# Retention plus two MoE layers on one core: one chunk's state products in a row, and the query decay multiplied into the output

## The chip, the cores and the metric

The kernel runs on one core of one Trainium2 chip. The metric is the device time of one execution in microseconds (us), the median of the runs shown. The engines are named as in the profile: PE is TensorE, PEld its weight loads, DVE is VectorE, ACT is ScalarE, POOL is GpSimd, SP is the engine that issues most loads.

## The reference, cut to what matters

Three layers follow each other: decayed attention ("retention") without softmax, an MoE-like layer with a rational activation, and a gated layer with RMS normalisation. The change lies in the first.

```python
batch, n_heads, seq, head_dim = (4, 8, 576, 64)
scores = scale * np.matmul(q, k.transpose(0, 1, 3, 2))
gamma = 1.0 - 2.0 ** (-5.0 - np.arange(H, dtype=np.float32))
Dmat = np.where(rel >= 0, gamma[:, None, None] ** rel[None, :, :], 0.0)   # rel = pos[:, None] - pos[None, :]
ret = scores * Dmat[None, :, :, :]
return np.matmul(ret, v)
```

The result, as 2304 tokens of 512 values, goes through `_moe_ref` (512 to 2048 to 512) and `_moe2_ref` (512 to 1536 to 512).

## The kernel before

The attention is cut into 20 steps: 4 batches (`b`) of 5 chunks (`c`), chunks 0 to 3 of 128 positions and chunk 4 of 64. Eight heads are held as four pairs (`p`), the two heads of a pair (`e`) on the two halves of the 128 partitions. The decay gamma^(i-j) is split in two powers. `prep_q` multiplies q in place by gamma^i (the table `gq`, with the scale in it), and `dmk` holds the mask times gamma^-j. A running state `SS` of each head carries all earlier chunks.

One step `i` of `att_jobs` issues:

- `att_add` (DVE, L280 or L278): adds the last chunk's state product out of PSUM to the state; `att_decay` (ACT, L227) makes the decayed copy for the chunk after.
- `att_scores` for step i+1, once for each `e` (PE, L202, four products): scores into a PSUM bank; DVE multiplies them by `dmk` into `ret` (L207).
- `att_out` (PE): for each pair a state product with 128 weight columns (L238, if c > 0) and then the two value products, with 64 weight columns each, into the two halves of the bank (L243). The first three chunks (the tokens of the first tile of the next layer) are split into two fp32r parts by ACT (L217) and DVE (L218); the other 17 are copied out of PSUM by ACT (L251) into `xe` and stored to DRAM by a DMA from ACT's queue (L252).
- `att_state` (PE, L264): the chunk's state product.
- `prep_q(i + 2)` on POOL (L188), and `prep_k(i + 1)` on POOL (L193), which multiplies k by its decay. `prep_q` of steps 0 and 1 is done by DVE at the start.

Every attention matmul is fp32, and the profile shows each as two instructions. Steps 0 to 2 run alone at the start (`att_jobs("h", 0, P0)`). The other 17 are spread over the first token tile of the second layer (`hook(j)`), between its own matmuls: `m1_up` (L312 to L314) and `m1_down` (L321, L322, L325), with their elementwise work on DVE, ACT and POOL (L331 to L369). In the same stretch the weights of that layer are unpacked from 64-bit floats (`Weights.step`): ACT L141 and L142, DVE L143, L144 and L148, POOL L151, ACT L157, and DVE or POOL L158; the result `w` is what `m1_up` and `m1_down` load. A scheduler that estimates times orders the instructions of each engine, so an edit in one place moves instructions in others. During the spread steps scores, output and state products take turns in two PSUM banks (`bank("a")`).

From 265 us on no attention work is left: the rest of the second layer and the third layer run.

## Time and profile before

| what | us |
|---|---|
| median of the runs | 1054.47 (1054.26 to 1058.04) |
| the profiled execution, its own time | 1060.39 |
| its span, first to last instruction | 1058.5 |
| PE busy / DVE busy / ACT busy / POOL busy, whole span | 1015.0 / 620.5 / 555.8 / 449.1 |
| granted TensorE clock, mean of the span | 0.954 |

How to read it: the shares of the whole span say little, since the attention lies in the first quarter only. There DVE is nearly as busy as PE, and the granted clock is well under 1. A PE that is "busy" at a granted clock of 0.5 (1.2 GHz) does half of what it does at 1.0 (2.4 GHz). A matmul's duration is a pipeline's latency: what a group of matmuls costs is read from the start of its first to the start of what comes after.

### The profile page before, as it was taken

The numbers are of one execution on the slowest core, as the hardware profiler recorded it, in microseconds if no ns is written. First come the engines' busy times: TensorE is split into PE (matmuls) and PEld (weight loads), VectorE is DVE, ScalarE is ACT, GpSimd is POOL, SyncE is SP. The second block draws the span as 40 slices with busy tenths as digits, with TensorE's granted clock in tenths as the row PEclk, the third lists the DMA queues.
The fourth block names the chain that finished last, engine by engine and source line by source line (L and its number), as shares of the span: only waits on it lengthen the run. The fifth ranks groups of instructions, "written<-read, shape, count | busy, mean of one in ns | idle before, by whom it ended". The sixth has DMA issues, their size and how long they took to land. (4 is left out here: it accounts for less than half of the span.)

```text
span 1058.5 us, 14977 instructions
## 1 busy us (share of the span) xinstructions
PE 1015.0 (96%) x5726; PEld 934.6 (88%) x5726; DVE 620.5 (59%) x1022; ACT 555.8 (53%) x1091; POOL 449.1 (42%) x397
## 2 busy tenths in 40 slices
PE   8988999989999999999999989898999999999998
PEld 6776877779999999999999889888999999999997
DVE  5598889896767768677688885765311211211211
ACT  2474566569778787787877665454311211211111
POOL 4474867577456474564755745554300100100000
PEclk7687889799999999999999999999999999999999
DMA  6554656431010010100102343332300100100000
GB/s 252 181 172 144 228 149 225 147 114 60 30 31 2 30 31 31 30 2 31 31 21 70 110 135 118 116 114 86 120 1 1 60 1 1 46 1 1 31 1 30
DMA packets 37592, 78.91 MB, mean 75 GB/s; under 512 B 5904, under 2 KB 21392, under 8 KB 37520
## 3 DMA queue, kind: packets, MB, share of 16 engines
q1 hardware_dynamic: 16416, 47.72, 13.5%
q10 hardware_dynamic: 21104, 30.23, 9.1%
q8 instruction: 45, 0.74, 0.3%
q14 instruction: 27, 0.22, 0.1%
HBM read 64.57 MB, written 13.37 MB: 74 GB/s over the span
## 5 line engine op out<-in xcount | busy, mean ns | idle before, releaser
L440 PE MATMUL bank<-x,w 128*128 128x384 f32 x528 | 178.4, 338 | 12.8 <-DVE sg L446 11.2
L442 PE MATMUL bank<-x,w 128*128 128x384 f32 x528 | 178.4, 338 | 0.0
L441 PE MATMUL bank<-x,w 128*128 128x384 f32 x528 | 178.2, 337 | 0.0
L446 DVE TENSOR_TENSOR sg<-sg,bank 128x384 f32<-128x384 f32 x72 | 39.8, 552 | 221.8 <-PE bank L442 221.6
L312 PE MATMUL bank<-x,w 128*128 128x384 f32 x384 | 134.3, 350 | 4.0 <-DVE u L350 4.0
L151 POOL TENSOR_TENSOR ft<-ft,raw 128x512 int32<-128x512 int32 x68 | 97.3, 1430 | 94.9 <-DVE ft L148 56.5
L348 POOL TENSOR_TENSOR q<-q,ah 128x384 f32<-128x384 f32 x96 | 101.9, 1062 | 81.8 <-ACT q L344 75.1
L322 PE MATMUL bank<-g,w 128*128 128x384 f32 x384 | 125.5, 347 | 7.9 <-DVE w L158 7.9
L314 PE MATMUL bank<-x,w 128*128 128x384 f32 x384 | 131.8, 343 | 0.6 <-DVE w L158 0.6
L313 PE MATMUL bank<-x,w 128*128 128x384 f32 x384 | 130.6, 340 | 0.0
L321 PE MATMUL bank<-g,w 128*128 128x384 f32 x384 | 125.1, 345 | 2.2 <-ACT g L368 1.1
L369 POOL TENSOR_TENSOR g<-u,g 128x384 fp32r<-128x384 f32 x96 | 101.3, 1056 | 60.1 <-ACT g L368 32.2
L218 POOL TENSOR_TENSOR x<-xr,x 128x384 fp32r<-128x384 f32 x44 | 47.8, 1096 | 162.9 <-ACT x L217 162.9
L440 PEld LDWEIGHTS bank<-x,w 128*128 128x128 f32 x528 | 99.9, 189 | 17.6 <-DVE sg L446 12.5
L445 ACT ACTIVATE sg<-bank 128x384 f32<-128x384 f32 x72 | 35.1, 488 | 143.8 <-PE bank L442 142.2
L441 PEld LDWEIGHTS bank<-x,w 128*128 128x128 f32 x528 | 99.9, 189 | 2.7
L442 PEld LDWEIGHTS bank<-x,w 128*128 128x128 f32 x528 | 100.0, 189 | 0.3
L448 ACT ACTIVATE y<-sg 128x384 fp32r<-128x384 f32 x72 | 37.6, 523 | 107.6 <-DVE sg L446 103.9
L325 PE MATMUL bank<-g,w 128*128 128x384 f32 x384 | 86.2, 341 | 0.0
L349 DVE TENSOR_TENSOR u<-u,bank 128x384 f32<-128x384 f32 x96 | 52.9, 551 | 52.4 <-ACT u L345 51.6
L322 PEld LDWEIGHTS bank<-g,w 128*128 128x128 f32 x384 | 73.8, 195 | 9.8 <-DVE w L158 9.5
L312 PEld LDWEIGHTS bank<-x,w 128*128 128x128 f32 x384 | 73.7, 192 | 8.4 <-DVE u L350 5.8
(101 smaller groups left out, 2210.8 us busy)
## 6 DMA issues: line engine op xcount, KB each, us to landing
raw<-in_w_out_dram SPq DMA_DIRECT2D x28, 512.0 KB, 3.5
xb<-in_qkT_dram ACTq DMA_DIRECT2D x17, 512.0 KB, 4.0
raw<-in_w_in_dram SPq DMA_DIRECT2D x16, 512.0 KB, 4.5
kv<-in_kv_dram ACTq DMA_DIRECT2D x14, 512.0 KB, 4.5
raw<-in_w_gate_dram SPq DMA_DIRECT2D x12, 512.0 KB, 3.5
raw<-in_w_val_dram SPq DMA_DIRECT2D x12, 512.0 KB, 3.5
xn_d<-x SPq DMA_DIRECT2D x6, 768.0 KB, 3.8
xr<-xn_d ACTq DMA_DIRECT2D x24, 192.0 KB, 2.4
```

The lines of the kernel that those rows point to most:

```text
L151: pool.tensor_tensor(out=ft, in0=ft, in1=lo, op=ALU.add)
L312: pe.matmul(out=h, lhsT=w[:, 0, ks], rhs=x[:, 0, k], start=(k == 0), stop=False)
L313: pe.matmul(out=h, lhsT=w[:, 0, ks], rhs=x[:, 1, k], start=False, stop=False)
L314: pe.matmul(out=h, lhsT=w[:, 1, ks], rhs=x[:, 0, k], start=False, stop=(k == KD - 1))
L321: pe.matmul(out=acc[m], lhsT=w[:, 0, ms], rhs=g[:, 0], start=(j == 0), stop=False)
L322: pe.matmul(out=acc[m], lhsT=w[:, 1, ms], rhs=g[:, 0], start=False, stop=False)
L325: pe.matmul(out=acc[m], lhsT=w[:, 0, ms], rhs=g[:, 1], start=False, stop=(j == J1 - 1))
L348: pool.tensor_tensor(out=q, in0=q, in1=ah, op=ALU.mult)
L369: pool.tensor_tensor(out=g[:, 1], in0=u, in1=g[:, 0].bitcast(F32), op=ALU.subtract)
L440: pe.matmul(out=t, lhsT=w[:, 0, ks], rhs=x[:, 0, k], start=(k == 0), stop=False)
L441: pe.matmul(out=t, lhsT=w[:, 0, ks], rhs=x[:, 1, k], start=False, stop=False)
L442: pe.matmul(out=t, lhsT=w[:, 1, ks], rhs=x[:, 0, k], start=False, stop=(k == KD - 1))
```

## The change

`prep_q` is gone: q stays as loaded, and so scores and the state product lack the factor gamma^i of their query position. The output lies with its positions along the free dimension as q did, so the factor is multiplied in where the output leaves PSUM: one DVE multiplication by `gq` out of the bank into `xe`. It takes the place of ACT's copy for 17 chunks, and stands ahead of the split for the first three. In `att_out` the four state products come first and then the eight value products. All groups of a chunk lie in one bank, and only the first product clears it.

```diff
-    def prep_q(i, eng):
-        if i < len(steps):
-            q = qk_b[i % 3][:, 0]
-            eng.tensor_tensor(out=q, in0=q, in1=gq, op=ALU.mult)
-
...
-        for p in range(NP):
-            if c > 0:
+        if c > 0:
+            for p in range(NP):
                 pe.matmul(
                     out=o[:, p, 0:n], lhsT=SS[c % 2][:, p].rearrange("p a d -> p (a d)"),
-                    rhs=q[:, p, 0:n], start=True, stop=False,
+                    rhs=q[:, p, 0:n], start=(p == 0), stop=False, skip_group_check=True,
                 )
+        for p in range(NP):
             for e in range(2):
                 pe.matmul(
                     out=o[64 * e:64 * e + 64, p, 0:n], lhsT=v[0:n, 2 * p + e],
-                    rhs=rets[i, e][0:n, p, 0:n], start=(c == 0), stop=True,
+                    rhs=rets[i, e][0:n, p, 0:n], start=(c == 0 and p == 0), stop=(p == NP - 1),
+                    skip_group_check=True,
                 )
         t0 = b * SEQ + c * CH
+        xo = xe[:, :, 0:n]
+        dve.tensor_tensor(out=xo, in0=o[:, :, 0:n], in1=gq[:, :, 0:n], op=ALU.mult)
         if t0 < TA:
-            split_x(0, slice(0, KD), t0, n, o[:, :, 0:n], dve)
+            split_x(0, slice(0, KD), t0, n, xo, dve)
         else:
-            act.activation(out=xe[:, :, 0:n], in_=o[:, :, 0:n], func=ACTF.Copy)
-            act.dma_start(out=x1_d[:, :, t0:t0 + n], in_=xe[:, :, 0:n])
+            act.dma_start(out=x1_d[:, :, t0:t0 + n], in_=xo)
...
-            prep_q(i + 2, pool)
             prep_k(i + 1, pool)
...
-    prep_q(0, dve)
...
-    prep_q(1, dve)
```

PE, step 2 of the start (`S_115` is the state, `ret` the masked scores, the second number a product's output). Before:

```order
L238 MATMUL bank_105<-xb,S_115 128x128
L243 MATMUL bank_105<-ret,kv_112 64x128 x2
L238 MATMUL bank_105<-xb,S_115 128x128
L243 MATMUL bank_105<-ret,kv_112 64x128 x2
L238 MATMUL bank_105<-xb,S_115 128x128
L243 MATMUL bank_105<-ret,kv_112 64x128 x2
L238 MATMUL bank_105<-xb,S_115 128x128
L243 MATMUL bank_105<-ret,kv_112 64x128 x2
```

PE, the same step after the change (L197 is the scores' line there, L262 the state product's, L233 and L239 what L238 and L243 were):

```order
L197 MATMUL bank_102<-xb 128x128 x4
L197 MATMUL bank_103<-xb 128x128 x4
L262 MATMUL bank_104<-kv_112 64x64 x8
L233 MATMUL bank_105<-xb,S_115 128x128 x4
L239 MATMUL bank_105<-ret,kv_112 64x128 x8
```

Seven changes between 128 and 64 weight columns have become one.

POOL at the start, before (L188 is the multiplication of q, L193 that of k, L151 a weight's unpacking):

```order
L188 TENSOR_TENSOR xb<-xb,gx 128x512
L193 TENSOR_TENSOR kv_112<-kv_112,gk 128x512
L151 TENSOR_TENSOR ft<-ft,raw 128x512
L188 TENSOR_TENSOR xb<-xb,gx 128x512
L151 TENSOR_TENSOR ft<-ft,raw 128x512
L193 TENSOR_TENSOR kv_110<-kv_110,gk 128x512
L188 TENSOR_TENSOR xb<-xb,gx 128x512
L151 TENSOR_TENSOR ft<-ft,raw 128x512
L188 TENSOR_TENSOR xb<-xb,gx 128x512
L151 TENSOR_TENSOR ft<-ft,raw 128x512
```

POOL there after the change (L188 is now k's multiplication):

```order
L188 TENSOR_TENSOR kv_111<-kv_111,gk 128x512
L188 TENSOR_TENSOR kv_112<-kv_112,gk 128x512
L151 TENSOR_TENSOR ft<-ft,raw 128x512 x2
L188 TENSOR_TENSOR kv_110<-kv_110,gk 128x512
L151 TENSOR_TENSOR ft<-ft,raw 128x512
L188 TENSOR_TENSOR kv_112<-kv_112,gk 128x512
L151 TENSOR_TENSOR ft<-ft,raw 128x512
```

The unpacking steps no longer stand behind a multiplication that waits for a load of q.

DVE after the change, around the third and fourth output (L246 is the new multiplication, L213 the split, L202 the scores' multiplication):

```order
L158 TENSOR_TENSOR w<-ft,w 128x512
L246 TENSOR_TENSOR gx<-bank_105,gx 128x512
L144 TENSOR_SCALAR ft<-ft 128x512
L202 TENSOR_TENSOR ret<-bank_102,dmk 128x512
L143 TENSOR_SCALAR ft<-ft 128x512
L148 SCALAR_TENSOR_TENSOR ft<-raw,ft 128x512
L202 TENSOR_TENSOR ret<-bank_105,dmk 64x4x64
L213 TENSOR_TENSOR x<-gx,x 128x4x128
L144 TENSOR_SCALAR ft<-ft 128x512
L246 TENSOR_TENSOR gx<-bank_104,gx 128x512
```

The bank now leaves by DVE, in line between a weight's steps and the scores.

## Rows read from the trace of the kernel before

**Rows 1.** Busy time by stretch: PE, PEld, DVE, ACT, POOL, PEclk, DMA share, GB/s.
```profile
0.00:47.00 47.00, 43.47 (x225) 30.49 (x225) 22.03 (x41) 16.87 (x34) 19.43 (x26) 0.64 0.62 217
47.00:240.00 193.00, 175.39 (x1206) 143.51 (x1204) 169.80 (x243) 120.20 (x240) 128.67 (x98) 0.87 0.54 172
...
265.00:558.00 293.00, 289.17 (x1649) 285.27 (x1648) 214.30 (x392) 228.09 (x457) 165.20 (x165) 1.00 0.08 26
```

**Rows 2.** Waits of PE, 47 to 265 us: total us, times, longest.
```profile
PE bank L322 <- DVE w L158: 7.9, 5, 3.3
PE bank L238 <- DVE S L280: 4.9, 3, 2.7
```

**Rows 3.** Waits of DVE, 47 to 240 us.
```profile
DVE ret L207 <- PE bank L202: 12.1, 9, 3.3
DVE S L280 <- PE bank L264: 4.3, 4, 1.4
```

**Rows 4.** Timeline of PE, step 2: start us, us; first rows of steps 2 and 3.
```profile
32.96 0.79 PE L238 MATMUL bank<-xb,S 128*128 128x128 f32 x2
...
38.37 0.80 PE L238 MATMUL bank<-xb,S 128*128 128x128 f32 x2
```

**Rows 5.** Timeline of PE, value products and scores each in a row.
```profile
14.51 1.97 PE L243 MATMUL bank<-ret,kv 128*64 128x128 f32 x16
16.41 2.07 PE L202 MATMUL bank<-xb 64*128 64x128 f32 x8
18.42 0.91 PE L264 MATMUL bank<-kv 128*64 128x64 f32 x12
```

**Rows 6.** Timeline of PE, a chunk at full clock and what follows it.
```profile
104.65 0.38 PE L238 MATMUL bank<-xb,S 128*128 128x128 f32 x2
...
107.69 0.67 PE L202 MATMUL bank<-xb 64*64 64x64 f32 x8
```

**Rows 7.** Groups by line and form, 0 to 420 us: count, busy us, mean ns, idle before.
```profile
L188 POOL TENSOR_TENSOR xb<-xb,gx 128x512 f32<-128x512 f32 x18 | 25.3, 1403 | 25.5 <-DMA xb<-in_qkT_dram 23.6 <-PE bank L202 1.3 <-DVE w L158 0.6
...
L207 DVE TENSOR_TENSOR ret<-bank,dmk 128x512 f32<-128x512 f32 x32 | 21.9, 686 | 23.7 <-PE bank L202 12.4 <-PE bank L243 8.2 <-POOL dmk L532 3.1
...
L251 ACT ACTIVATE gx<-bank 128x512 f32<-128x512 f32 x13 | 7.7, 590 | 11.5 <-PE bank L243 11.5
...
L207 DVE TENSOR_TENSOR ret<-bank,dmk 64x256 f32<-64x256 f32 x8 | 3.3, 414 | 2.4 <-PE bank L202 2.3
...
L218 DVE TENSOR_TENSOR x<-bank,x 128x512 fp32r<-128x512 f32 x3 | 2.1, 684 | 0.0
```

**Rows 8.** The same view: DVE operations with and without a PSUM operand.
```profile
L148 DVE SCALAR_TENSOR_TENSOR ft<-raw,ft 128x512 int32<-128x512 int32 x32 | 30.4, 950 | 0.6
...
L144 DVE TENSOR_SCALAR ft<-ft 128x512 int32<-128x512 int32 x32 | 25.9, 808 | 0.5
...
L158 DVE TENSOR_TENSOR w<-ft,w 128x512 fp32r<-128x512 f32 x24 | 25.4, 1060 | 1.8 <-ACT w L157 1.8
...
L332 DVE SCALAR_TENSOR_TENSOR bank<-q,bank 128x384 f32<-128x384 f32 x42 | 23.5, 559 | 0.7
...
L332 DVE SCALAR_TENSOR_TENSOR q<-q,ah 128x384 f32<-128x384 f32 x16 | 16.1, 1007 | 0.1
```

**Rows 9.** Line L144 alone, 0 to 265 us: duration ns, shortest, median, longest.
```profile
L144 DVE TENSOR_SCALAR ft<-ft x32: 410/724/1498, 15.7 to 231.5; 128x512 int32<-128x512 int32 x32
```

**Rows 10.** Timeline of POOL: a multiplication of q that waits, and what follows.
```profile
43.27 1.27 POOL L188 TENSOR_TENSOR xb<-xb,gx 128x512 f32<-128x512 f32 x1 [6.53 <-DMA xb<-in_qkT_dram]
44.50 1.30 POOL L151 TENSOR_TENSOR ft<-ft,raw 128x512 int32<-128x512 int32 x1
```

**Rows 11.** Two stretches at half clock, columns as in rows 1.
```profile
17.00:27.00 10.00, 10.00 (x53) 7.86 (x52) 6.12 (x10) 2.12 (x5) 5.12 (x4) 0.50 0.41 118
187.00:200.00 13.00, 12.49 (x48) 10.05 (x49) 9.58 (x14) 7.24 (x15) 7.48 (x6) 0.50 0.44 160
```

**Rows 12.** Stores from L252: us from issue to landing.
```profile
DMA to landing us min/median/max: 2.2/3.7/6.3
```

**Rows 13.** Timeline of PE: first matmul of the second layer.
```profile
42.99 0.67 PE L312 MATMUL bank<-x,w 128*128 128x384 f32 x1
```

## Prediction

> **What bounds the kernel now.** I first cut the span by stage with the busy times by stretch [rows 1], since the change touches only the attention, which ends before 265 us. From 265 to 558 us PE is busy 289.17 of 293.00 us at a granted clock of 1.00: that stretch is PE's own and the change leaves its work alone. Of the two stretches with attention, the first (0 to 47 us) is PE's too: PE is busy 43.47 us while DVE is busy 22.03 and ACT 16.87, at a clock of 0.64. The second (47 to 240 us) belongs to nobody alone: PE is busy 175.39 of 193.00 us, so idle 17.6, and DVE 169.80, so idle 23.2. The waits say the same from both sides: PE waits for unpacked weights (7.9 us) and for the state's addition (4.9 us) [rows 2], and DVE waits for scores (12.1 us) and state products (4.3 us) [rows 3]. In such a stretch a saving on one engine reaches the end only in part, and work added to DVE costs in part.
>
> **PE: the products in a row.** In step 2, at half clock, the state products start at 32.96 and those of step 3 at 38.37, so a chunk of four state and eight value products takes 5.41 us [rows 4]. Without state products between them the eight value products take 16.41 - 14.51 = 1.90 us, and four score products, which also load 128 weight columns, 18.42 - 16.41 = 2.01 us [rows 5]. Four state products in a row are not in the trace. The score products are the nearest row, so a chunk would take 2.01 + 1.90 = 3.91 us, which is 1.50 less. As a bound from the other side, if alternating cost nothing the saving would be zero, but then rows 4 and 5 could not differ by 1.50, so I leave a loss out. At full clock a chunk takes 107.69 - 104.65 = 3.04 us [rows 6]; the saving lies between half of 1.50 (it scales with the clock) and 1.50, and I take 0.9, near the half, because 3.04 itself is nearer to half of 5.41 than to all of it.
>
> Sixteen of the twenty chunks have state products: twelve of 128 positions and four of 64. Three of the twelve fall in the first stretch, at half clock: 3 x 1.50 = 4.5 us. The other nine lie between 47 and 240 us, where the mean clock is 0.87 [rows 1]; at 1.1 us each that is 9.9 us. For the four short ones no row shows the parts; they get half, 0.6 us each, 2.4 us. So PE loses 4.5 us of work at the start and 12.3 us in the mixed stretch.
>
> **POOL: no multiplication of q.** Eighteen operations of 1403 ns go, 25.3 us [rows 7]. POOL is not the bound (128.67 of 193.00 us), but two things hang on it. First, these operations wait for loads of q, 23.6 us in all [rows 7], and what is queued behind them waits too: at 43.27 us one has waited 6.53 us for its load, and a weight's unpacking step runs only after it, at 44.50 [rows 10]. That step leads to the weights for which PE waits 7.9 us [rows 2]. I give back 3 us of these 7.9; the bounds are 0 and 7.9.
>
> Second, POOL's work lengthens DVE's. L144 takes between 410 and 1498 ns for the same shape [rows 9]. The same L332 takes 559 ns with a PSUM operand and 1007 ns with both in SBUF [rows 8]. Against 410 ns for L144, 559 for L332 and, for the two-operand lines L148 and L158 of 128x512, the 686 ns of L207 [rows 7], the surplus is 32 x 398 + 16 x 448 + 32 x 264 + 24 x 374 ns = 12.7 + 7.2 + 8.4 + 9.0 = 37.3 us. The removed 25.3 us are 17% of POOL's 19.43 + 128.67 us [rows 1]; by that share DVE gets 6.4 us back, some 5.4 of them after 47 us.
>
> The Trainium skill ("SBUF — State Buffer", section "Who interferes with whom") says that VectorE operations with two SBUF inputs, or in a two-port mode, and GpSimd operations that read SBUF lock each other out for a whole instruction. Rows 8 and 9 agree in kind. If every removed operation had blocked DVE for its whole length, 25.3 us instead of 6.4 would come back, and the forecast below would be some 8 us lower.
>
> **DVE: the multiplication out of PSUM.** It has one PSUM and one SBUF operand, as L207 has in the same shape: 686 ns, and 414 ns for the 64-position form [rows 7]. Sixteen full and four short ones make 11.0 + 1.7 = 12.6 us, less two multiplications of q at the start. Four full ones fall before 47 us, where DVE has 25 us idle; they cost nothing as long as that idle time lasts. After 47 us DVE gets 8.2 + 1.7 = 9.9 us, less the 5.4 above: 4.5 us net. The three splits (L218, 684 ns) now read SBUF twice and can take up to L158's 1060 [rows 8], 1.1 us more, also in idle time. The first three outputs reach the second layer one operation (0.69 us) later; chunk 2's products end before 38.37 [rows 4] and the first L312 runs at 42.99 [rows 13], so 4.6 us cover it. If the scheduler uses up this cover, it costs 0.7 us.
>
> **ACT and the store.** ACT loses thirteen copies of 590 ns [rows 7] and four short ones; it is busy 120.20 of 193.00 us, so this alone gives nothing. The store's issue stays in ACT's queue and now waits there for DVE; behind it stand ACT's weight steps, so a late DVE multiplication holds them up. The next multiplication writes the same `xe`, so it has to wait for the store: 2.2 to 6.3 us to land [rows 12], against some eleven us from chunk to chunk (17 of them in 193 us). Free, as long as ACT issues the store within 5 us.
>
> **The sum.** Start: -4.5. Mixed stretch: half of PE's 12.3, -6.2 (half, because the idle times 17.6 and 23.2 say that each engine is the late one about as often); half of DVE's added 4.5, +2.3; weights earlier, -3. Together -11.4 us. The profiled execution took 1060.39 us (span 1058.5 and 1.9 around it), which gives 1049.0; it is 5.9 above the median of the runs, 1054.47, from which the forecast is 1043 us.
>
> **Rivals.**
>
> 1. *PE is the bound throughout, and the clock follows.* For it: PE runs at a clock of 0.50 from 17 to 27 us although it is never idle there [rows 11], so denser products might raise the clock. Against it: the scores in a row there [rows 5] did not. All of PE's 16.8 us and the 7.9 us of waits for weights would give 1054.5 - 24.7 = 1030. A few us less if some stretch like 187 to 200 us (13 us at 0.50 [rows 11]) ran at full clock.
>
> 2. *DVE is the bound, and PE's saving turns into waiting.* For it: DVE is busy 88% of the mixed stretch. Then only the start's 4.5 us remain, and the added work counts whole: with POOL's relief +4.5, without +9.9. 1054.5 to 1060, so about no change.
>
> 3. *The bank leaves late, and the clock falls: slower.* The output's bank is now emptied by DVE, in line behind weight steps of up to 1.5 us [rows 9], and not by ACT, which was there at once (its 11.5 us of waiting before L251 were for PE [rows 7]). With two banks in turn, the next state product waits for it. It decides from the point where the multiplication comes later than the matmuls placed between output and state product can cover, some 3 us. Each such wait can be followed by a stretch like that at 187 us, where 13 us at half clock [rows 11] cost up to 6.5. Two of them and waits of 2 us at each, +17, less the start's 4.5 and plus DVE's 2.3: 1069. Against it: the order puts the multiplications early in DVE's row, one or two operations after the products.
>
> The Trainium skill ("TensorEngine Tiling (Array Packing)", section "PSUM Bottleneck") advises emptying PSUM with both ScalarE and VectorE, because faster products do not empty it faster. The change does the opposite for 17 chunks. By that rule the third rival would hold and give its 1069; the row of L251 shows ACT waiting for PE, not PE for ACT, so I keep it at a small chance.
>
> **How the numbers follow.** A difference under 0.5% (5.3 us) can hardly be told from none in a measurement of this kernel. The forecast (1037 to 1049) gets 0.50, the first rival (1028 to 1037) 0.25, the second 0.15, the third 0.10. Faster by over 0.5%, under 1049.2: 0.75; within: 0.15; slower: 0.10. The range 1029 to 1056 leaves out the end of the first rival (0.05), part of the second and the third, together about 0.2.
>
> **What would show it.** In the profile of the changed kernel: the state products of a step within 2.0 us at half clock or 1.1 us at full, and the chunk in under 2.2 us at full clock; the new multiplication at about 686 ns; L144's median under 724 ns; POOL some 25 us less busy; no wait of PE's state products for DVE; the attention ending some 11 us earlier, and the time after it unchanged. Wrong would be: a chunk that still takes 3 us, DVE busy above 95% of the stretch, or more stretches at a clock of 0.50 than before.

## The result, and the profile after

The changed kernel takes 1028.26 us (median of 4 runs, 1024.55 to 1032.28) against 1056.26 us of the kernel before beside it: a ratio of 0.973, 95% interval 0.968 to 0.978. It is faster by 28 us where 11.4 were forecast, and ends just under the range's lower end of 1029. The profiled execution took 1024.55 us, its span 1022.8 us at a mean granted clock of 0.984 (before: 0.954). Of either kernel a run's time goes with its mean clock (before: 1045 us at 0.970, 1065 us at 0.947), so the experiments below give medians of all runs, and beside them the recorded ratio with its interval; for e1, e2, e3 and e5 that ratio sets them against the runs of the kernel before under 1060 us, for the others against runs that are 1055 to 1061 us in the mean, so the ratios do not all stand on one footing.

The busy times by stretch of the changed kernel (columns as in [rows 1]):

```profile
0.00:47.00 47.00, 42.33 (x348) 33.29 (x350) 35.58 (x63) 27.29 (x54) 21.85 (x27) 1.00 0.81 287
47.00:240.00 193.00, 171.68 (x1269) 154.18 (x1266) 177.01 (x286) 131.24 (x261) 124.46 (x100) 0.93 0.51 159
265.00:558.00 293.00, 287.77 (x1643) 284.28 (x1642) 217.41 (x393) 231.34 (x463) 174.99 (x170) 1.00 0.11 34
```

In the first 47 us PE runs 348 matmul instructions instead of 225 in about the same busy time, since the clock stays at 1.00 instead of 0.64. In the mixed stretch the clock is 0.93 instead of 0.87, and DVE, not PE, is now the busier engine (177.01 of 193.00 us).

PE's timeline of the changed kernel, a short chunk (64 positions) and a full one, both at full clock; L233 and L239 are the state and value products, L197 is the next group:

```profile
38.96 1.00 PE L233 MATMUL bank<-xb,S 128*128 128x64 f32 x8
39.88 0.68 PE L239 MATMUL bank<-ret,kv 64*64 64x64 f32 x16
40.50 0.71 PE L197 MATMUL bank<-xb 64*128 64x128 f32 x4
...
59.88 1.05 PE L233 MATMUL bank<-xb,S 128*128 128x128 f32 x8
60.87 1.09 PE L239 MATMUL bank<-ret,kv 128*64 128x128 f32 x16
61.89 1.16 PE L197 MATMUL bank<-xb 64*128 64x128 f32 x8
```

A full chunk takes 61.89 - 59.88 = 2.01 us where it took 3.04 [rows 6]. Waits of PE in the changed kernel, 47 to 265 us (total us, times, longest):

```profile
PE bank L197 <- DVE ret L202: 6.4, 5, 2.8
PE bank L319 <- DVE w L158: 5.3, 4, 3.6
PE bank L262 <- DVE gx L246: 3.1, 3, 1.6
PE bank L318 <- ACT w L157: 2.4, 3, 0.9
```

Waits of DVE there, 47 to 240 us:

```profile
DVE u L346 <- ACT u L342: 10.3, 3, 5.2
DVE q L328 <- ACT bank L359: 1.7, 2, 1.1
...
DVE ret L202 <- PE bank L197: 0.4, 1, 0.4
```

The two sides have changed places: DVE waited 12.1 us for scores [rows 3] and now waits 0.4; PE waits for DVE's masked scores, for its weights, and a little (3.1 us) for the new multiplication. What DVE waits for now is ACT.

DVE's groups by line and form in the changed kernel (count, busy us, mean ns, idle before):

```profile
L148 DVE SCALAR_TENSOR_TENSOR ft<-raw,ft 128x512 int32<-128x512 int32 x32 | 25.9, 809 | 0.3
L143 DVE TENSOR_SCALAR ft<-ft 128x512 f32<-128x512 f32 x32 | 24.1, 753 | 0.9 <-ACT ft L141 0.8
...
L158 DVE TENSOR_TENSOR w<-ft,w 128x512 fp32r<-128x512 f32 x24 | 21.4, 890 | 1.2 <-ACT w L157 1.2
...
L246 DVE TENSOR_TENSOR gx<-bank,gx 128x512 f32<-128x512 f32 x16 | 10.9, 680 | 0.8 <-PE bank L239 0.7
```

L144 alone (shortest, median, longest ns):

```profile
L144 DVE TENSOR_SCALAR ft<-ft x32: 410/419/1542, 15.2 to 196.5; 128x512 int32<-128x512 int32 x32
```

The new multiplication takes 680 ns as costed. L148 fell from 950 to 809 ns, L158 from 1060 to 890, and L144's median from 724 to 419 [rows 8, 9]. Not all got shorter: L143 rose from 641 to 753.

**Where the time went.** I measure up to a fixed point of the work behind the attention, the first product with `ones` of the third layer's sums of squares; what comes after it took the same before and after (786.5 and 786.3 us of the span). The row from the start to that point, of the kernel before:

```profile
0.00:271.97 271.97, 249.71 (x1599) 204.12 (x1599) 214.05 (x326) 164.98 (x328) 169.71 (x145) 0.84 0.50 163
```

and of the changed kernel:

```profile
0.00:236.52 236.52, 210.52 (x1594) 184.25 (x1595) 209.15 (x341) 156.51 (x310) 145.30 (x126) 0.94 0.58 187
```

Such a row splits the time on PE into three: idle (271.97 - 249.71 = 22.3 us), what the clock takes (271.97 x (1 - 0.84) = 43.5), and the rest, PE's work at full clock (206). After: 26.0, 14.2 and 196. So of 35.5 us between the two profiles the clock gave 29, PE's work 10, and PE's waiting took 4 back. The same sum over whole runs, time x (1 - mean clock): 47 to 52 us in the kernel before, 25 in the changed one (medians of the comparisons below). **Most of the gain is clock.** This split counts where the time went; what moved the clock is the question of the experiments.

### The profile page after: what moved, and what is told of

Read it like the earlier page. It is cut to its first block, busy times and chain, and to the rows that moved or that the text cites. A ratio compares the mean times of both kernels' runs of the same rounds, so it can differ in the third digit from the quotient of the medians.

```text
span 1022.8 us, 14979 instructions
## 1 busy us (share of the span) xinstructions
PE 974.8 (95%) x5726; PEld 911.9 (89%) x5726; DVE 613.5 (60%) x1040; ACT 547.7 (54%) x1074; POOL 424.5 (42%) x379
## 3 DMA queue, kind: packets, MB, share of 16 engines
q1 hardware_dynamic: 16416, 47.72, 14.2%
## 4 chain that ended last, share of the span: by engine, by line
PE 63%; DVE 18%; ACT 5%; issue 5%; DMA 5%; POOL 4%; ACTq 0%; DVEq 0%; POOLq 0%
PE bank L437 7%; PE bank L439 7%; PE bank L438 7%; PE bank L319 5%; PE bank L322 5%; PE bank L309 5%; PE bank L311 5%; PE bank L310 5%; PE bank L318 4%; PE bank L455 4%; PE bank L454 4%; PE bank L456 4%; DVE ft L148 3%; DVE ft L143 3%; DMA raw<-in_w_val_dram 2%
## 5 line engine op out<-in xcount | busy, mean ns | idle before, releaser
L437 PE MATMUL bank<-x,w 128*128 128x384 f32 x528 | 178.3, 338 | 12.1 <-DVE sg L443 9.0
L151 POOL TENSOR_TENSOR ft<-ft,raw 128x512 int32<-128x512 int32 x68 | 97.5, 1435 | 106.0 <-DVE ft L148 59.1
L345 POOL TENSOR_TENSOR q<-q,ah 128x384 f32<-128x384 f32 x96 | 102.2, 1065 | 73.2 <-ACT q L341 72.9
L366 POOL TENSOR_TENSOR g<-u,g 128x384 fp32r<-128x384 f32 x96 | 100.8, 1052 | 69.6 <-issue 35.5
L437 PEld LDWEIGHTS bank<-x,w 128*128 128x128 f32 x528 | 99.4, 188 | 18.4 <-DVE sg L443 10.7
L213 POOL TENSOR_TENSOR x<-xr,x 128x384 fp32r<-128x384 f32 x44 | 48.1, 1107 | 154.0 <-ACT x L212 154.0
L438 PEld LDWEIGHTS bank<-x,w 128*128 128x128 f32 x528 | 99.4, 188 | 2.6
L439 PEld LDWEIGHTS bank<-x,w 128*128 128x128 f32 x528 | 99.4, 188 | 0.5 <-POOL w L158 0.2
L445 ACT ACTIVATE y<-sg 128x384 fp32r<-128x384 f32 x72 | 37.6, 523 | 109.0 <-DVE sg L443 106.7
L319 PEld LDWEIGHTS bank<-g,w 128*128 128x128 f32 x384 | 72.9, 193 | 7.2 <-DVE w L158 6.7
L318 PEld LDWEIGHTS bank<-g,w 128*128 128x128 f32 x384 | 71.6, 190 | 8.1 <-ACT w L157 3.2
```

Of the source, the lines that this page charges most:

```text
L151: pool.tensor_tensor(out=ft, in0=ft, in1=lo, op=ALU.add)
L318: pe.matmul(out=acc[m], lhsT=w[:, 0, ms], rhs=g[:, 0], start=(j == 0), stop=False)
L319: pe.matmul(out=acc[m], lhsT=w[:, 1, ms], rhs=g[:, 0], start=False, stop=False)
L345: pool.tensor_tensor(out=q, in0=q, in1=ah, op=ALU.mult)
L366: pool.tensor_tensor(out=g[:, 1], in0=u, in1=g[:, 0].bitcast(F32), op=ALU.subtract)
L437: pe.matmul(out=t, lhsT=w[:, 0, ks], rhs=x[:, 0, k], start=(k == 0), stop=False)
```

## The experiments

The kernels, their medians, the median of the kernel before on the same chip, the ratio with its interval, and what the clock takes of a run (this kernel / before, median of the runs):

| kernel | us | before, us | difference | ratio | clock takes, us |
|---|---|---|---|---|---|
| changed, again (e0) | 1032.24 | 1059.88 | -27.6 | 0.971 [0.967, 0.975] | 25 / 49 |
| changed, third (e17) | 1032.78 | 1062.01 | -29.2 | 0.973 [0.965, 0.981] | 25 / 52 |
| e1: order only | 1045.22 | 1061.31 | -16.1 | 0.993 [0.990, 0.997] | 33 / 50 |
| e2: decay only | 1050.64 | 1061.31 | -10.7 | 0.993 [0.987, 1.000] | 41 / 50 |
| e3: before, filled wait | 1065.42 | 1061.31 | +4.1 | 1.016 [1.011, 1.021] | 47 / 50 |
| e14: before without q's multiplication | 1040.56 | 1057.41 | -16.9 | 0.978 [0.966, 0.990] | 30 / 47 |
| e13: changed without its multiplication | 1025.29 | 1057.41 | -32.1 | 0.969 [0.963, 0.976] | 21 / 47 |
| e5: changed, POOL's operation kept | 1046.49 | 1061.31 | -14.8 | 0.995 [0.991, 0.999] | 36 / 50 |
| e10: changed, POOL only touches q | 1032.64 | 1059.88 | -27.2 | 0.972 [0.968, 0.976] | 26 / 49 |
| e4: multiplication twice | 1051.68 | 1059.88 | -8.2 | 0.997 [0.991, 1.003] | 41 / 49 |
| e12: half in a row | 1037.57 | 1057.41 | -19.8 | 0.982 [0.976, 0.988] | 30 / 47 |
| e15: state products twice | 1039.65 | 1062.01 | -22.4 | 0.980 [0.972, 0.988] | 23 / 52 |
| e8: changed, filled wait | 1030.16 | 1057.41 | -27.3 | 0.976 [0.970, 0.981] | 20 / 47 |
| e11: more weights on POOL | 1026.81 | 1059.88 | -33.1 | 0.968 [0.965, 0.971] | 23 / 49 |
| e16: e8 and e11 | 1032.21 | 1062.01 | -29.8 | 0.975 [0.968, 0.983] | 21 / 52 |

Median and ratio differ most for e1, e2, e3 and e5, on one chip, where the kernel before spread from 1045 to 1066 us over 25 runs. By the ratios e1, e2, e4 and e5 each lie within 2% of the kernel before. Differences between kernels of different chips are rougher, by either measure, than those beside each other.

The changed kernel was run beside others twice more:

> The changed kernel itself, beside the kernel before on this chip, so that the runs of this call have their measure. After the first comparison: 1024 to 1034 us, 0.973 of the kernel before; start at a granted clock of 1.00, first matmul of the second layer at 28.7 us, attention end near 183 us.

> The changed kernel once more, as the measure of the two runs beside it on this chip: 1024 to 1034 us, mean clock 0.972 to 0.985.

Both came out as expected in time. The start did not: in both the clock fell once ahead of the second layer, for 13.7 and 10.2 us, and the first matmul of that layer came at 33.0 and 31.6 us, not at 28.7. The profile shown above is the changed kernel at its best.

### The two halves of the change

Order alone, in the kernel before (the loop of the state products ahead of the loop of the value products, as in the change):

> The kernel before with the state products of a chunk in a row ahead of its value products, and nothing else: q is still multiplied on POOL, the bank still leaves by ACT. Clock theory (the denser products keep the granted clock up): the start runs at 1.0, the first matmul of the second layer comes at 29 to 33 us instead of 42.99, and the whole is 18 to 24 us faster. Rival, POOL and DVE relief (the gain came from q's multiplication leaving POOL): PE's own 9 to 12 us at most, and fewer if the clock stays at 0.5 in the start. Rival, the first wait alone (the clock falls because of PE's idle time at 10 to 12 us, whatever the products): the start stays at 0.5, first matmul of the second layer at 38 to 39 us, 6 to 11 us faster.

The clock fell at 12.7 us here too, but for 13.7 us instead of 34, and the second layer's first matmul came at 34.70 us, not at 29 to 33 as the clock theory had it. The time was 16 us shorter by the medians, between that theory's 18 to 24 and its rival's 9 to 12 at most (PE's own work), and 7 by the ratio, which is the rival's.

All but that, the old alternation with the new decay:

> The changed kernel with the old order of products (a state product, its two value products, and so on): the query decay is multiplied into the output by DVE, POOL does not touch q. Clock theory: the start stays at 0.5 and the whole is within 6 us of the kernel before. POOL and DVE relief: 12 to 20 us faster than before, with the weights earlier. Rival, the first wait alone: PE's wait for q's multiplication in the first microseconds is gone here as in the changed kernel, so the start runs at 1.0 and the first matmul of the second layer comes near 32 us; 8 to 14 us faster.

The start was the clock theory's: down for 37.6 us, the second layer's first matmul at 45.37. The time was neither theory's: 11 us under before by the medians, 7 by the ratio. PE's wait ahead of the fall had not gone (1.75 us), so the third theory was not put to a test.

Then the decay was taken apart. Without `prep_q` and with nothing in its place:

```diff
-            prep_q(i + 2, pool)
...
-    prep_q(0, dve)
...
-    prep_q(1, dve)
```

> The kernel before without the multiplication of q on POOL and on DVE at the start, and nothing in its place (that decay power is left out of the result, so part of the computation is missing; the old order of the products stays). This shows POOL's relief alone. Theory A, a POOL operation takes its own length from DVE (15 us of POOL took 14 us from DVE in the run with the operation put back) and DVE's time counts whole: 14 to 20 us under the kernel before, and DVE's total to the end of the stretch 14 us shorter. Theory B, as the prediction sized it: 3 us for the weights that come earlier and half of 6.4 us of DVE, 6 us under it.

And the same with the products in a row, which is the changed kernel with ACT's copy in the place of the multiplication:

> The changed kernel without its multiplication out of PSUM: ACT copies the bank as before (the decay power of the query's position is left out of the result altogether, so part of the computation is missing). This shows what DVE's new 12.6 us cost by themselves. Theory A, DVE's time in the mixed stretch counts whole or more (doing the multiplication twice cost 19 us): 12 to 19 us under the changed kernel. Theory B, it counts half as the prediction took it: 5 to 6 us under it. Theory C, PE bounds the stretch now and the multiplication lies in its shadow (the second one only went over the edge): under 3 us.

With these each part is measured twice, in the presence and in the absence of the others (differences of the ratios of medians, in us): the order -16 (e1), -15 (e13 against e14) and -17 (changed against e2); POOL's operation gone -17 (e14) and -16 (e13 against e1); the new multiplication +6 (e2 against e14) and +4 (changed against e13). The sum -16 - 17 + 5 = -28 is what the change brought; that it comes out is no evidence, since along either path the differences add up to it by construction. What is evidence is that two paths give like sizes. By the ratios the order is -0.7% (e1), -0.8% (e13 against e14) or -2.1% (changed against e2), so that its size is known only as 7 to 22 us (the 22 from kernels on different chips); POOL's part is -2.2% (e14) and -2.4% (e13 against e1), large by both; the new multiplication is +1.6% (e2 against e14) and +0.2 to 0.4% (changed against e13), 2 to 16 us. By the ratios the halves do not add up: e1 and e2 have 7 us each, the whole 28. How much of the gain comes only with both together is open. For e14 the row to the fixed point shows that DVE is 214.05 - 199.23 = 14.8 us less busy than before, as theory A had it (two multiplications of q at the start, 1.4 us, among it), while POOL is 169.71 - 141.10 = 28.6 us less busy:

```profile
0.00:250.08 250.08, 234.37 (x1586) 190.69 (x1587) 199.23 (x320) 162.19 (x323) 141.10 (x125) 0.90 0.55 177
```

e13's -4 us stands nearest to theory B, the half that the prediction took, but its interval (0.963 to 0.976) holds the changed kernel's ratio, so theory C is not excluded.

e13's timeline also shows a chunk in a row at half clock, which the trace of before did not have:

```profile
23.29 2.07 PE L238 MATMUL bank<-xb,S 128*128 128x128 f32 x8
25.29 1.98 PE L244 MATMUL bank<-ret,kv 128*64 128x128 f32 x16
27.20 2.08 PE L202 MATMUL bank<-xb 64*128 64x128 f32 x8
```

27.20 - 23.29 = 3.91 us, the prediction's figure.

### Why POOL's operation cost 17 us

The changed kernel with a multiplication of q by one left on POOL, in the old place:

```diff
+            eng.tensor_tensor(out=q, in0=q, in1=one, op=ALU.mult)
...
+            same_q(i + 2, pool)
```

> The changed kernel, with a multiplication of q by one kept on POOL where the kernel before had its multiplication by the decay (from step 2 on), so that POOL has the same work, the same waits for q's loads and the same lock-outs of DVE as before. POOL and DVE relief: most of the gain goes, 1045 to 1052 us. Clock theory: 3 to 8 us of the gain go, 1031 to 1037 us, and the start still runs at 1.0. By the prediction's own terms (3 us for earlier weights, half of 5.4 us of DVE) 6 us go.

And with the same operation on two positions of each pair only, so that POOL still waits for q's load and the scores still hang on POOL:

> The changed kernel with a POOL operation on q put back in its old place, but on 128x4x2 elements instead of 128x512: POOL waits for the loads of q as before and the scores still hang on POOL, but POOL is busy for almost nothing. The full-size operation in that place cost 13 to 18 us (the run before this). Theory A, POOL's time and what it takes from DVE cost it: this kernel is within 4 us of the changed kernel, attention end near 184 us, first matmul of the second layer near 29 us. Theory B, the waiting for loads at the head of POOL's queue and the scores that hang on POOL cost it: 12 to 18 us above the changed kernel, attention end near 197 us, as with the full-size operation. In between: both.

e10 takes the changed kernel's time; e5, by the medians, loses 12 us of the gain. So the scores' dependence on POOL shows no cost; POOL's busy time does. The wait at the head of POOL's queue is hardly tested: the operation waited 1.6 us for loads of q in e10 and 3.6 in e5, against 23.6 in the kernel before [rows 7]. The group of that operation in e5 (columns as in [rows 7]):

```profile
L189 POOL TENSOR_TENSOR xb<-xb,ones 128x512 f32<-128x512 f32 x18 | 22.5, 1248 | 9.7 <-DMA xb<-in_qkT_dram 3.6 <-DMA kv<-in_kv_dram 3.5 <-DVE ret L208 2.5
```

L144 alone in e5, shortest, median and longest ns:

```profile
L144 DVE TENSOR_SCALAR ft<-ft x32: 410/682/1532, 14.8 to 219.6; 128x512 int32<-128x512 int32 x32
```

The row from the start to the fixed point in e5:

```profile
0.00:255.00 255.00, 220.57 (x1609) 190.88 (x1610) 228.21 (x345) 157.83 (x312) 167.27 (x146) 0.92 0.51 174
```

The same three views of e10, the group:

```profile
L189 POOL TENSOR_TENSOR xb<-xb,ones 128x8 f32<-128x8 f32 x18 | 8.8, 490 | 8.1 <-DVE ret L208 5.6 <-DMA xb<-in_qkT_dram 1.6 <-DVE ft L144 0.8
```

L144 alone:

```profile
L144 DVE TENSOR_SCALAR ft<-ft x32: 409/416/1490, 17.6 to 205.6; 128x512 int32<-128x512 int32 x32
```

And the row to the fixed point:

```profile
0.00:243.00 243.00, 217.50 (x1595) 190.30 (x1595) 208.89 (x341) 156.72 (x310) 153.27 (x144) 0.91 0.55 182
```

POOL is busy 167.27 - 153.27 = 14.0 us longer in e5, and DVE, with the same work but for four more operations, 228.21 - 208.89 = 19.3 us. In this pair a microsecond of POOL takes a microsecond of DVE or somewhat more; in e14 against the kernel before it takes half of one (14.8 for 28.6 us). PE's idle time goes from 25.5 to 34.4 us with it (as in e1, where it is 34).

### What DVE's own work costs

The multiplication done twice:

```diff
+        dve.tensor_tensor(out=xo, in0=o[:, :, 0:n], in1=gq[:, :, 0:n], op=ALU.mult)
```

> The changed kernel with the new DVE multiplication out of PSUM done twice for every chunk (sixteen at about 686 ns and four at 414 ns more, 12.6 us of DVE). Theory A, DVE's work in the mixed stretch counts in half, as the prediction took it: 5 to 6 us above the changed kernel. Theory B, DVE bounds the stretch: 10 to 13 us above it. Theory C, PE bounds it and DVE has room: under 3 us above it. If the clock falls because of it (one more stretch of 13 us at 0.50), 6 us more than each of these.

The second multiplication, 12.5 us of DVE, costs 1051.68 - 1032.24 = 19.4 us, where the first one costs 4 to 6 by the medians. e4's longest waits of PE, 0 to 265 us:

```profile
PE bank L197 <- DVE ret L202: 11.4, 12, 2.2
PE bank L320 <- DVE w L158: 8.4, 5, 3.3
PE bank L310 <- DVE u L348: 4.5, 3, 2.8
```

Its row to the fixed point:

```profile
0.00:262.64 262.64, 227.34 (x1606) 199.58 (x1607) 215.59 (x363) 157.84 (x311) 145.27 (x127) 0.88 0.50 169
```

PE idles 35.3 us instead of 25 (e0: 243.29 - 218.68 = 24.6), and over the run the clock takes 41 us instead of 25. Theory B with one more fall of the clock, 16 to 19 us, comes nearest; the falls follow waits of PE (next section). DVE's time has no fixed price here.

### What the clock follows

Filling the first wait with three more warm-up products, in the kernel before and in the changed one:

```diff
+    for i in range(3):
+        pe.matmul(out=banks[0], lhsT=warm[:, 0:128], rhs=warm, start=True, stop=True)
```

> The kernel before with three more 128x512 warm-up products behind the five that it has, so that PE is not idle while the masks are made; all else as before. The first wait alone: the granted clock stays at 1.0 through the start, the first matmul of the second layer comes at 31 to 34 us instead of 42.99, 8 to 12 us faster. Clock theory (only the denser products hold the clock): the clock falls in the start in spite of it and the whole is within 4 us of the kernel before. POOL and DVE relief says nothing of the start, and expects no change.

> The changed kernel with three more warm-up products behind the first scores, in the wait for k's multiplication on POOL that precedes the first state product (2.3 us in the run whose clock fell to 0.50 at 11 us and stayed there 13.7 us, 0.24 us in the one whose clock did not fall). Theory A, this wait makes the clock fall: no fall at the start in any profile, and the median 1024 to 1028, that of the changed kernel's faster runs. Theory B, the wait has nothing to do with it: the clock falls as before, and the median stays at 1028 to 1034. In the kernel before the same filling did nothing for the clock (it fell at 16.6 us, after the second state product).

Neither helped: the clock fell at 16.6 us and stayed down to 54 in e3, and it fell at 14.8 us for 10 us in e8. But neither is a test, because the wait was not filled. It moved behind the added products: PE idles from 13.27 to 14.82 us in e3 and from 12.38 to 13.96 in e8, and the fall came behind it. (In e16, with the same products, the wait was 0.6 us long and the clock did not fall.) All profiles together (one of each kernel; the loss is half of the later time at half clock, up to the fixed point) show what the start depends on:

| profiles | state products | PE idle, 6 to 17 us | clock down at the start, us | clock's loss after it, us |
|---|---|---|---|---|
| before, e2, e3, e14 | alternating | 1.5 to 2.1 | 34.1, 37.6, 37.6, 41.0 | 25.6, 27.3, 22.2, 3.4 |
| e0, e1, e4, e8, e10, e11, e12, e15, e17 | in a row (e12 half) | 1.3 to 2.5 | 10.2 to 13.7 | 10.2 to 25.6 |
| e13 | in a row | 2.1 | 23.9 | 11.9 |
| changed (first), e5, e16 | in a row | 0.3 to 0.6 | 0 | 13.7, 20.5, 13.7 |

The row of that stretch, first of the kernel before, then of the first changed one:

```profile
6.00:17.00 11.00, 8.91 (x63) 6.57 (x62) 5.34 (x10) 4.29 (x10) 7.84 (x12) 0.80 0.97 374
6.00:17.00 11.00, 10.36 (x92) 7.38 (x90) 5.69 (x11) 4.47 (x10) 5.95 (x11) 1.00 1.05 398
```

In these profiles the clock's fall at the start goes with PE's wait there, and how long it then stays down with the order. The alternation does not hold it down so long in every run: e14's fastest lost 1024.84 x (1 - 0.989) = 11 us to the clock in the whole, less than the 20.5 us (half of 41.0) that its profile lost at the start alone. Half of the alternation:

```diff
-            for p in range(NP):
+        for h in (0, 2):
+            if c > 0:
+                for p in (h, h + 1):
...
+            for p in (h, h + 1):
```

> The changed kernel with its products half in a row: two state products, four value products, two state, four value, so three changes between 128 and 64 weight columns in a chunk instead of one (and seven before). If the cost goes with the changes, each is (3.04 - 2.01) / 6 = 0.17 us at full clock and a chunk takes 2.35 us there. Theory A, the changes between the two kinds also let the clock fall and keep it down at the start: time at 0.50 ahead of the second layer's first matmul between the changed kernel's (0 to 13.7 us) and the old order's (31 to 38 us), and the whole a third of the way from the changed kernel to the one with the old order (which was 10 us under before): 1034 to 1044 us on a chip where before takes 1060. Theory B, only the time of the changes counts and the clock does as chance has it: 16 x 0.34 = 5 us at most, 1032 to 1038 us, with the clock at the start as in the changed kernel.

A chunk at full clock, from its first state product to what follows:

```profile
77.32 0.71 PE L234 MATMUL bank<-xb,S 128*128 128x128 f32 x4
...
79.78 0.48 PE L197 MATMUL bank<-xb 64*128 64x128 f32 x2
```

It took 79.78 - 77.32 = 2.46 us (estimate 2.35), the start behaved as in the changed kernel (theory B), and the time lies 20 us under before, half of the way from the changed kernel (28) to the old order (e2, 11). At 1037.57 us it is in the ranges of both theories, so the time does not decide.

Last, PE got back the work that the row order saves, but without the alternation:

```diff
-            for p in range(NP):
+            for p in [*range(NP), *range(NP)]:
```

> The changed kernel with the four state products of a chunk issued twice in a row (the second time over the first, so the result stays). This gives PE back about the work that the row order took away: 12 x 1.08 us and four short ones of half that, some 15 us at full clock, with one change of weight columns in a chunk as before. In the runs so far the time went with what the clock takes (time x (1 - mean clock)): 49 us in the kernel before, 26 in the changed one. Theory A, the many changes between the two kinds of product hold the clock down: here they are few, so the clock stays as in the changed kernel (0.97 to 0.98 in the mean, time at 0.50 ahead of the second layer's first matmul under 25 us), and the time rises only by PE's 15 us less what its waits cover: 1034 to 1046. Theory B, the clock rose because PE had less to do: the mean clock falls back to 0.955 to 0.96 and the time to 1052 to 1062, that of the kernel before.

The row of e15 to the fixed point:

```profile
0.00:253.79 253.79, 231.99 (x1726) 204.17 (x1727) 209.89 (x344) 157.86 (x311) 145.06 (x127) 0.92 0.54 175
```

PE's work is back (253.79 less 21.8 idle less 20.3 for the clock leaves 212 us, before 206, changed 196), yet the clock takes 23 us of a run as in the changed kernel, not 52, and the time is 22 us under before. So it is not less work that raised the clock. At the start, in the profiled runs, it is the alternation that held it down; for the time after it, see below. e15 costs 6.9 us over e17 beside it, for 15 us of products.

Rows at the start agree. PE in the kernel before, steps 1 and 2, never idle:

```profile
25.00:34.00 9.00, 9.00 (x58) 7.06 (x56) 3.61 (x7) 3.48 (x8) 2.54 (x3) 0.50 0.46 146
```

and in the changed kernel (e17), where the clock had fallen as well, and came back during the first state and value products:

```profile
12.00:22.00 10.00, 10.00 (x62) 8.85 (x62) 8.56 (x14) 4.95 (x10) 2.58 (x3) 0.55 0.71 265
25.00:34.00 9.00, 8.93 (x98) 7.24 (x95) 8.92 (x18) 6.20 (x15) 3.56 (x3) 1.00 0.83 264
```

In the four profiles with the old order (before, e2, e3, e14) the clock was down from 12 to 17 us until 46 to 54 us; in the thirteen with the new one (e12 among them) it came back by 36 us at the latest, and in three of them it did not fall at the start (the table above).

In the mixed stretch most falls follow a wait of PE, whatever the order. In the kernel before, PE waits 2.75 us for the state in the first of these stretches, and the clock is at 0.50 in the next, though PE is never idle there:

```profile
84.00:91.00 7.00, 4.25 (x41) 3.50 (x39) 6.95 (x10) 2.53 (x7) 5.46 (x4) 1.00 0.57 178
91.02:101.26 10.24, 10.24 (x53) 7.77 (x52) 5.98 (x11) 5.75 (x13) 3.51 (x3) 0.50 0.67 195
```

The changed kernel has such falls too:

```profile
195.00:202.16 7.16, 3.89 (x21) 3.24 (x19) 7.12 (x9) 4.49 (x10) 5.13 (x5) 1.00 0.29 82
202.16:208.99 6.83, 5.54 (x17) 5.54 (x18) 3.40 (x5) 2.50 (x5) 6.23 (x6) 0.50 0.53 182
```

A chunk of 64 positions that alternates does it without a wait. In e2, PE is busy all through the first of these stretches, which ends with such a chunk (175.02 to 177.42 us):

```profile
171.00:178.00 7.00, 7.00 (x53) 6.37 (x52) 6.90 (x15) 4.59 (x10) 2.65 (x3) 1.00 0.58 204
178.00:186.00 8.00, 7.67 (x43) 6.36 (x41) 6.61 (x10) 2.97 (x6) 6.87 (x6) 0.57 0.96 339
```

Of 17 falls up to the fixed point in before, e2 and e14, four came with no wait of PE in the 5 us ahead (0.1 us at most), and each of the four with an alternating chunk of 64 positions there; of 27 in the changed kernel (first profile and e17), e4 and e15, in all PE had idled, 0.5 to 3.6 us of these 5 and 2.0 in the mean; their other stretches of 5 us at full clock have 0.4 in the mean. So two things lower the clock here, alternation and waiting.

After the start the change does not remove the waits: PE idles 24.6 to 26.1 us up to the fixed point instead of 22.3, and the clock falls six times, as before. What differs is how long it stays down, 4.6 to 5.7 us in the mean of a fall instead of 8.5. The order alone does not explain that: e3 and e14 keep the alternation and have short falls too (4.9 and 3.4 us), and e14, without POOL's operation, loses the least of all to the clock after the start (3.4 us). Why the clock comes back sooner in the mixed stretch, about 8 to 12 of the some 25 us, stays open.

### Is there a better version?

With every second instead of every fourth of the last unpacking steps on POOL, and with that and the filled wait together:

```diff
-dve if wa.n1 % 4 else pool
+dve if wa.n1 % 2 else pool
```

> The changed kernel with every second instead of every fourth of the last unpacking steps (w from ft and w, line 158 there) on POOL instead of DVE: part of the room that the change left on POOL is used up again, and DVE is relieved by about 1.06 us for each that moves, some eight of them. If DVE bounds the mixed stretch: 4 to 8 us under the changed kernel. If POOL's time is what cost 13 to 18 us in the run with q's multiplication put back (18 operations, 25 us): 8 operations of about 1.4 us cost 5 to 8 us, less what DVE gets back: between no change and 6 us slower. If PE and its clock bound it: within 3 us.

> The changed kernel with both small steps that looked no worse: every second of the last unpacking steps on POOL instead of every fourth, and three more warm-up products behind the first scores. If each takes off what it seemed to (5 us and 2 us): 1021 to 1026. If both were within the noise of single kernels' clocks: 1025 to 1033, as the changed kernel.

e11 is 5.4 us under the changed kernel beside it, but the intervals touch, and e16 is level with it (1032.21 and 1032.78). No better version is shown. Moving an operation from DVE to POOL does not relieve DVE: its time to the fixed point is 208.84 us in e11, 209.15 in the changed kernel's first profile and 207.55 in e0.

## Why the prediction was wrong, point by point

**The row order's own price: right.** A chunk at half clock takes 3.91 us as worked out, at full clock 2.01 us; 0.9 us were taken as the saving and 1.03 measured. The short chunk takes 1.54 us (40.50 - 38.96); in e2, which keeps the old order, it takes 121.96 - 119.56 = 2.40 at full clock, so it saves 0.86 where 0.6 was taken:

```profile
119.56 0.33 PE L233 MATMUL bank<-xb,S 128*128 128x64 f32 x2
...
121.96 1.16 PE L197 MATMUL bank<-xb 64*128 64x128 f32 x8
```

**The clock as a constant: the step that failed.** "Three of the twelve fall in the first stretch, at half clock: 3 x 1.50 = 4.5 us" and "between 47 and 240 us, where the mean clock is 0.87" priced the change at the clock of before. But the clock was no constant. At the start of the profiled runs the alternation held it down, and the change saved there not 4.5 us but 9 to 14: the second layer's first matmul went from 42.99 [rows 13] to 28.7 to 33.8 us (changed kernel three times, and e10), and the first 47 us from 0.64 to 1.00 or, in e0, 0.85. The order alone has 8.3 of that in e1 and 3.0 in e13 against e14 (37.36 and 40.35 us). Over a run the clock took some 25 us less, and the sum has no term for it.

The first rival named this ("the clock follows", 1028 to 1037, at 0.25). It was right that the clock rises, and wrong that PE is the bound throughout: PE idles 26.0 us up to the fixed point. Its 1030 was added up from all of PE's 16.8 us and 7.9 us of waits, with the clock as "a few us" more, so that the measured time lies beside it is luck. What spoke against it, that scores in a row at 17 us did not raise the clock, was no evidence: in e17 the same scores are at half clock too, and the clock comes back only with the state and value products in a row.

**Half of PE's saving reaches the end: not shown, its size luck.** In the changed kernel 10 us of PE's work went and 4 came back as waiting. With the order alone (e1) PE's work to the fixed point falls from 206 to 197 us and its idle time rises from 22.3 to 34.0, so that all the saved work turned into waiting, in part for DVE; what reached the end was clock. The prediction's -10.7 us for both stretches lies within the 7 to 22 us that the order measured, but the reason is another one.

**POOL: the mis-sized term.** "By that share DVE gets 6.4 us back" and 3 us for earlier weights, together -5.7 us in the sum; measured -16 to -17 by the medians, -2.2 to -2.4% by the ratios. The share treated POOL's 17% as 17% of a surplus of 37.3 us. Measured, DVE got back not 6.4 us but 13 (e14, 14.8 less the two multiplications of q), half of the time that POOL lost; e5 against e10 has it whole. And DVE's lateness costs PE waits (9 us) and then clock (10 us) as well, as e5 and e10 show. The other half, that q's loads hold up POOL's queue [rows 10], is not measured by itself: without that operation's own time, e10's 1.6 us of such waits cost nothing that shows.

The Trainium skill ("SBUF — State Buffer", section "Who interferes with whom") says that VectorE operations with two SBUF inputs, or in a two-port mode, and GpSimd operations that read SBUF lock each other out for a whole instruction. The traces agree in kind, in size in one of two: 14.0 us more of POOL and 19.3 us more of DVE (e5 against e10), but 28.6 and 14.8 (before against e14). By that rule the prediction named a forecast 8 us lower, 1035, nearer to the time measured; DVE's own time came back to 13 us, between the share's 6.4 and the rule's 25.3.

**DVE's multiplication: right in its length.** 680 and 414 ns; +4 to +6 us for it by the medians, where half of 9.9 us was taken, but 2 to 16 by the ratios. That this half is no constant, e4 shows.

**ACT, the store: right.** No wait for the store is among DVE's between 47 and 240 us in the changed kernel. Not foreseen: ACT's L342 is what DVE waits for now.

**The other rivals.** DVE as the bound with PE's saving lost (1054 to 1060) is nearly what happens when DVE gets 12.5 us more (e4, 1052). The bank that leaves late is seen, at 3.1 us of PE's waits, and the time is far from that rival's +17; by the rule that the prediction weighed there (the Trainium skill, "TensorEngine Tiling (Array Packing)", section "PSUM Bottleneck") the time would have been 1069, and the trace does not agree: DVE alone emptied the bank at the price of those 3.1 us.

**The signs.** As foretold came the chunk (2.01 us), the new multiplication (680 ns), L144's median (419 ns), POOL's time (24.4 us less up to the fixed point) and the unchanged rest. Two did not: the state products do wait for DVE (L262 for L246, 3.1 us), and the attention ends at 182.8 us instead of 226.4, 44 us earlier and not 11.

## What to carry to other kernels

When PE runs at half clock without being idle, the clock is part of what an edit changes: look at what runs there (here fp32 products that alternate between 128 and 64 weight columns) before pricing the edit at that clock. An operation on POOL beside a busy DVE is to be counted as DVE's time as well, here for half of its length up to the whole, and a wait of PE as one that a stretch at half clock may follow. Compare whole distributions with their clocks where runs of one kernel spread over 2%.

## What the runs showed of the hardware that I had not expected

- The clock was at 0.50 for 9.00 us of a PE that was busy for 9.00 us, on alternating fp32 products, and came back to 1.00 on the same products sorted; twice as many state products in a row (e15) kept it as high as once.
- At the start the clock did not fall in the three profiles in which PE idled 0.3 to 0.6 us between 6 and 17 us, and fell in all fourteen with 1.3 to 2.5 us; it then stayed down for 10.2 to 23.9 us with the state products in a row and for 34.1 to 41.0 with the alternation.
- A POOL multiplication of 128x8 elements takes 490 ns, against 1248 ns for 128x512 (e10, e5).
- The first 12.6 us of DVE's work out of PSUM cost 4 to 6 us by the medians, the next 12.5 us cost 19.4.
